# Lightning attention feeding a sine MLP: the start of the first chunk and the end of the second chunk's attention put in another order

## The chip, the cores and the metric

The kernel runs on one core of a Trainium2 chip. The time is what the device takes for one launch, in microseconds, as the median of several runs. Five engines work side by side, each through its own instructions in order: TensorE (PE, matmuls and transposes; PEld is its weight load), VectorE (DVE), ScalarE (ACT), GpSimd (POOL) and SyncE (SP). TensorE writes only to PSUM, eight banks of 2 KB per partition; DVE and ACT read results out of it. Transfers between memory and the on-chip buffers (SBUF) are issued from the queues of POOL and SP.

## What is computed

Block-wise linear attention over 4 batches x 8 heads x 768 positions x 64 values, with a decay per head, and then a two-layer MLP on the 3072 rows of 512 values that come out. Cut to what matters:

```python
for b in range(nb):                       # blocks of positions, state carried along
    intra = einsum('bhic,bhjc->bhij', qb, kb) * Dmask
    intra = einsum('bhij,bhjd->bhid', intra, vb)
    inter = einsum('bhid,bhde->bhie', qb * lam_pow, kv_state)
    out[:, :, sl] = intra + inter
    kv_state = lam_block * kv_state + einsum('bhsd,bhse->bhde', kb * rev_pow, vb)
x = out.transpose(0, 2, 1, 3).reshape(3072, 512)
h = x @ w_in                              # 512 -> 2048
g = h + sin(alpha * h)**2 / (alpha + 1e-09)
return g @ w_out                          # 2048 -> 512
```

## The kernel before

**Chunks and units.** The kernel takes 128 positions at a time: six chunks `t`, and four batches in each, so 24 units `u = 4*t + b`. Units 0 to 3 are the first chunk, 4 to 7 the second. The attention of chunk g+1 is worked in between the MLP of chunk g, so that both fill the engines.

**One unit's attention.** `transposes(u)` (L173) turns k and q with eight small matmuls, and ACT copies both out in one operation (`QKT`, L183). `scores(u)` (L196) makes k times q with eight matmuls into `F_ps` (two banks, tag `pf`), and DVE multiplies by the mask and writes `STm` (L209). `intra_mm(u)` (L244) multiplies `STm` with v into `O_ps`, `inter_mm(u)` (L254) adds the carried state, and `copy_x(u)` (L261, DVE) multiplies by the table `Etab` and writes the unit's columns of `xt`, the input of the MLP. `part_fo(uf, uo)` (L405) issues intra of `uo`, scores of `uf` and inter of `uo`, in this order. In the first chunk there is no carried state, and `first_out` (L345) stands in for intra, inter and copy.

**The MLP of one chunk** is cut into sixteen parts `f` of 128 columns. `hidden(g, f)` (L278) issues four matmuls of 512 columns into one bank, then ACT takes the sine (L286) and, for odd f and all f above 7 in chunk 0 and for every f later, the square (L289). `finish(g, f)` (L292) issues the DVE operation that makes `gall` (L296), which is also what frees the bank. `project(g, n)` (L305) is a quarter of an output tile, four matmuls of 512 columns: n runs over 16 pairs of (batch m, quarter), by `ORDER`. The first four of them come ahead of the next chunk's first `hidden`, the others between its parts. `hidden(1, 0)` reads `xt` of all four units 4 to 7.

**What sets the order.** The schedule is written by hand: each engine gets its instructions in the order in which the code issues them. `slots(0)` (L426) says after which `hidden(0, f)` which attention work of units 4 to 7 is issued, and the block under `if g == 0` (L503) issues what is left behind f = 15, with the first four `project` calls. `feed` (L452) does the same for POOL. PSUM banks go by tag: `pqk`, `po`, `ops`, `h0`, `h1`, `h2` of one bank each and `pf` of two; the next user of a tag waits for the reader of the one before. Chunk 0's hidden parts go through `FIRST` (`h0 h2 po h1 ops h0 h2 h1 ops` for f = 0 to 8) and then `h{f%3}`.

**The start.** k and q of unit 0 come through SP (`kraw`, `qraw`) and are cast by DVE (L334, L341). k, q and v of units 1 to 3 come through POOL's queue one by one (`load`, L85), then `w_in` in five pieces, then chunk 1 in halves (units 4 and 5, then 6 and 7). `spin(n)` (L356) issues n matmuls on a constant tile that nothing reads, into the bank of tag `h0`. `make_identity` (L110, L126) builds identity matrices with POOL; the small one, `idf`, serves the transpose of `alpha` (`a_ps`).

Of the kernel before, what the change touches and what calls it, by code (L numbers as in the profile page):

```python
# [15 lines left out]
def kernel(  # L16
# [15 lines left out]
    T = 128  # L32
# [90 lines left out]
            load(0, i, bi, bi + 1)  # L123
    load(0, 2, B - 1, B)
    idf = consts.tile([NFC, NFC], FP32, name="idf")
    make_identity(nc, idf[:])  # L126
    for i in range(4):
        load_w_in(i)
    new_chunk(1)
# [43 lines left out]
    def transposes(u, tag="pqk"):  # L173
        t, b = divmod(u, B)
        QK_ps = psA.tile([P, 2, HP, T], BF16, name="QK_ps", tag=tag)
        for hp in range(HP):
            nc.tensor.transpose(out=QK_ps[:, 1, hp, :],
                                in_=kn[t][:, b, 2 * hp:2 * hp + 2, :], identity=iden[:])
        for hp in range(HP):
            nc.tensor.transpose(out=QK_ps[:, 0, hp, :],  # L180
                                in_=qn[t][:, b, 2 * hp:2 * hp + 2, :], identity=iden[:])
        QKT = qkp.tile([P, 2, HP, T], BF16, name="QKT")
        nc.scalar.copy(out=QKT[:], in_=QK_ps[:])  # L183
        st[u]["QT"], st[u]["KT"] = QKT[:, 0, :, :], QKT[:, 1, :, :]
# [8 lines left out]
            for n in range(2):  # L193
                st[u + n][nm] = XT[:, n, :, :]

    def scores(u, halves=1):  # L196
        QT, KT = st[u]["QT"], st[u]["KT"]
        F_ps = psA.tile([P, 2, HP, T], FP32, name="F_ps", tag="pf")
        for hp in range(HP):
            for hd in range(2):  # L200
                nc.tensor.matmul(out=F_ps[:, hd, hp, :],  # L201
                                 lhsT=KT[hd * D:(hd + 1) * D, hp, :],
                                 rhs=QT[hd * D:(hd + 1) * D, hp, :],
                                 start=True, stop=True)
        STm = work.tile([P, 2, HP, T], BF16, name="STm")
        n = HP // halves
        for s in range(halves):
            w = slice(s * n, (s + 1) * n)
            nc.vector.tensor_tensor(out=STm[:, :, w, :], in0=F_ps[:, :, w, :], in1=Cmask[:, :, w, :],  # L209
                                    op=ALU.mult)  # L210
        st[u]["STm"] = STm

    def state_mm(us, tag="pqk"):
# [27 lines left out]
            nc.gpsimd.tensor_tensor(out=kvd[b][:], in0=kvs[u][:],  # L241
                                    in1=L128[:].unsqueeze(2).broadcast_to([P, HP, D]), op=ALU.mult)

    def intra_mm(u):  # L244
        t, b = divmod(u, B)
        O_ps = psA.tile([P, HP, T], FP32, name="O_ps", tag="po")
        for hp in range(HP):
            for hd in range(2):
                nc.tensor.matmul(out=O_ps[hd * D:(hd + 1) * D, hp, :],  # L249
                                 lhsT=vn[t][:, b, 2 * hp + hd, :], rhs=st[u]["STm"][:, hd, hp, :],  # L250
                                 start=(hp == 0), stop=False, skip_group_check=True)
        st[u]["O_ps"] = O_ps
# [8 lines left out]
    def copy_x(u):  # L261
        t, b = divmod(u, B)
        nc.vector.tensor_tensor(out=xt[t][:, :, b * T:(b + 1) * T], in0=st[u]["O_ps"][:], in1=Etab[:],  # L263
                                op=ALU.mult)
# [80 lines left out]
    def first_out(u, tag, hps_=range(4)):  # L345
        O_ps = psA.tile([P, HP, T], FP32, name="O_ps", tag=tag)
        for hp in hps_:
            for hd in range(2):
                nc.tensor.matmul(out=O_ps[hd * D:(hd + 1) * D, hp, :],
                                 lhsT=vn[0][:, u, 2 * hp + hd, :], rhs=st[u]["STm"][:, hd, hp, :],  # L350
                                 start=True, stop=True, skip_group_check=True)
        w = slice(hps_[0], hps_[-1] + 1)
        nc.vector.tensor_tensor(out=xt[0][:, w, u * T:(u + 1) * T], in0=O_ps[:, w, :],
                                in1=Etab[:, w, :], op=ALU.mult)

    def spin(n, cols=512):  # L356

        ps = psA.tile([P, GRP], FP32, name="hps", tag="h0")
        for _ in range(n):
            nc.tensor.matmul(out=ps[:, 0:cols], lhsT=fill[:, 0:P], rhs=fill[:, 0:cols], start=True, stop=True)  # L360

    spin(9)
    for nm, src, tag in (("KT", kn, "pqk"), ("QT", qn, "ops")):
        X_ps = psA.tile([P, HP, T], BF16, name="X_ps", tag=tag)
        for hp in range(HP):
            nc.tensor.transpose(out=X_ps[:, hp, :], in_=src[0][:, 0, 2 * hp:2 * hp + 2, :], identity=iden[:])
        XT = qkp.tile([P, HP, T], BF16, name=nm + "0")
        nc.scalar.copy(out=XT[:], in_=X_ps[:])
        st[0][nm] = XT[:]
        spin(3)  # L370
    scores(0)
    spin(1)
    transposes(1, "pqk")
    for hp in range(HP):
        nc.scalar.activation(out=Etab[:, hp, :], in_=pos_row[:], func=ACTF.Exp, scale=ln_hd[:, hp:hp + 1])
    spin(2)
    transposes(2, "ops")
    warm = consts.tile([P, 1], FP32, name="warm")
    nc.scalar.activation(out=warm[:], in_=lnlam[:, 0:1], func=ACTF.Sin)
    spin(1)  # L380
    scores(1)
    spin(1)
    first_out(0, "po")
    spin(1)
    scores(2)
    a_ps = psA.tile([P, NFC], FP32, name="a_ps", tag="h2")
    nc.tensor.transpose(out=a_ps[:], in_=alpha_fp[:], identity=idf[:])
    transposes(3, "pqk")
    spin(2)
    first_out(1, "h1")  # L390
    alpha_sb = consts.tile([P, NFC], FP32, name="alpha_sb")
    nc.vector.tensor_copy(out=alpha_sb[:], in_=a_ps[:])
    r_sb = consts.tile([P, NFC], FP32, name="r_sb")
    nc.vector.reciprocal(out=r_sb[:], in_=alpha_sb[:])
    spin(2)
    scores(3, 2)
    spin(1)
    first_out(2, "po")
    spin(2)
    first_out(3, "h1", range(0, 2))  # L400
    first_out(3, "ops", range(2, 4))
    spin(3)


    def part_fo(uf, uo, tag=None):  # L405

        if uo is not None:
            if tag:
                state_mm([uo], tag)
            intra_mm(uo)  # L410
        if uf is not None:
            scores(uf)
        if uo is not None:
            inter_mm(uo)
            if tag:
                state_put(uo)
                state_decay(uo)
# [8 lines left out]
    def slots(g):  # L426

        u = [B * (g + 1) + b for b in range(B)]
        T_, FO = transposes, part_fo
        if g == 0:  # L430
            return {3: [(part_k, (0, 1), "pf")], 6: [(part_k, (2, 3), "pf")],
                    7: [(T_, u[0])], 8: [(T_, u[1], "po")], 9: [(FO, u[0], None)],
                    11: [(FO, u[1], u[0]), (copy_x, u[0])], 12: [(T_, u[2])],
                    13: [(FO, None, u[1]), (T_, u[3], "ops"), (copy_x, u[1])], 14: [(FO, u[2], None)]}, {}
        if g == 1:
            return {4: [(part_k, (4, 5), h_tag(1, 5))], 6: [(part_k, (6, 7), h_tag(1, 7))],
                    8: [(FO, u[0], None)], 10: [(FO, u[1], u[0], h_tag(1, 11))],
                    12: [(FO, u[2], u[1], h_tag(1, 13))],
                    14: [(FO, u[3], u[2], h_tag(1, 15)), (copy_x, u[2])],
                    15: [(FO, None, u[3], h_tag(2, 0)), (copy_x, u[3])]}, {10: u[0], 12: u[1]}  # L440
        at = (3, 6, 9, 12, 14) if g == 2 else (1, 4, 7, 10, 13)
        tg = [h_tag(g, f + 1) if g < NT - 2 else None for f in at[1:]]
        return {at[0]: [(FO, u[0], None)], at[1]: [(FO, u[1], u[0], tg[0])], at[2]: [(FO, u[2], u[1], tg[1])],
                at[3]: [(FO, u[3], u[2], tg[2])], at[4]: [(FO, None, u[3], tg[3])]}, \
               {at[n + 1]: u[n] for n in range(4)}
# [30 lines left out]
    for g in range(NT + 1):  # L476
        if g < NT:
            gall[g] = gbp.tile([P, NFC, GRP], BF16, name="gall")
        at, xs = slots(g) if g + 1 < NT else ({}, {})
        fd = feed(g) if g + 1 < NT else {}  # L480
        if g + 1 < NT:
            new_xt(g + 1)
        for i in range(NFC):
            if g == NT and i >= NFC - 4 - LEAD:
                break
            for a in fd.get(i, []):
                if a is not None:
                    a[0](*a[1:])
            if g < NT:
                hidden(g, i)  # L490
            for a in at.get(i, []):
                a[0](*a[1:])
            if g > 0:
                n = i + LEAD
                if n < NFC:
                    project(g - 1, n)
                elif g < NT:
                    project(g, n - NFC)
            if g < NT:
                finish(g, i)  # L500
            if i in xs:
                copy_x(xs[i])
        if g == 0:  # L503

            project(0, 0)
            part_fo(7, 6)
            copy_x(6)
            project(0, 1)
            project(0, 2)
            part_fo(None, 7)  # L510
            copy_x(7)
            project(0, 3)
    project_halves(NT - 1, B - 1)

# [29 lines left out]
```

## Time and profile before

| what | us |
|---|---|
| median of 3 runs (lowest to highest) | 218.99 (218.78 to 219.08) |
| the profiled execution, its own time | 219.22 |
| its span on the core | 217.5 |
| PE busy | 208.3 (96%) |
| ACT busy | 147.2 (68%) |
| DVE busy | 126.6 (58%) |
| POOL busy | 94.3 (43%) |
| first matmul of hidden(0, 0) | at 18.48 |
| first matmul of hidden(1, 0) | at 46.26 |
| granted TensorE clock | 1.00 |

The times of the views count from the start of the span. A line of the timeline gives start, duration, engine, line of the kernel, operation, output and inputs with their shapes, how many were merged, and in brackets how long the engine stood idle before it and what ended that. A line of the chain gives start, duration and what it was; the chain is followed back from the last instruction, at each step to what released it. A line of the stretches gives the busy time of each engine with its number of instructions, the granted clock, and the transfers. A matmul's recorded duration holds its drain, so one following another starts before the first one's record ends.

### The profile page before, as it was taken

To read this page: it belongs to the slowest core of one execution; us is meant where nothing else is said; L and a number is where in the kernel's file an instruction comes from. 1 tells how busy PE (TensorE), PEld (TensorE's weight loads), DVE (VectorE), ACT (ScalarE), POOL (GpSimd) and SP (SyncE) were. 2 spreads that over 40 slices of the span, in tenths; PEclk is the share of its full clock that TensorE was granted. 3 is DMA by queue.
4 is the path that set the end of the run, shared out by engine and by line. 5 is a ranking of instruction groups with operands and counts; after the bars stand their busy time and mean duration, and the time that the engine had idled before them with its cause. 6 is when DMAs were issued, how large, how long until landed. Compare 5 with 4: busy or idle time off the path is not lost.

```text
span 217.5 us, 3864 instructions
## 1 busy us (share of the span) xinstructions
PE 208.3 (96%) x1504; PEld 99.6 (46%) x1504; DVE 126.6 (58%) x183; ACT 147.2 (68%) x234; POOL 94.3 (43%) x131
## 2 busy tenths in 40 slices
PE   7799986999999999999999999999999999999994
PEld 2354443544444544445454444444444444444453
DVE  4576977834656875567656777545767544444300
ACT  5573998728766648766667675777676779787521
POOL 7999999963899569052474611100000000000000
PEclk9999999999999999999999999999999999999999
DMA  5999999999999999929689990490110101111022
GB/s 102 150 158 198 176 167 184 208 175 154 197 176 136 177 148 139 189 46 135 143 101 124 166 119 29 116 128 21 75 50 3 48 0 48 51 50 48 0 101 96
DMA packets 99747, 24.65 MB, mean 113 GB/s; under 512 B 91904, under 2 KB 96784, under 8 KB 99728
## 3 DMA queue, kind: packets, MB, share of 16 engines
q0 software_dynamic: 76976, 13.37, 79.0%
q1 hardware_dynamic: 22752, 11.03, 23.6%
q8 instruction: 12, 0.20, 0.4%
q14 instruction: 7, 0.06, 0.1%
HBM read 27.28 MB, written 6.29 MB: 154 GB/s over the span
## 4 chain that ended last, share of the span: by engine, by line
PE 78%; POOL 10%; DMA 5%; ACT 2%; issue 2%; DVE 1%; POOLq 0%; ACTq 0%
PE ops L311 36%; PE hps L283 32%; DMA qn<-in_q_dram 5%; PE O_ps L257 3%; PE F_ps L201 2%; POOL vn L87 2%; PE O_ps L249 2%; POOL kdec L170 2%; POOL qn L87 2%; POOL w_in L93 2%; PE KVA_ps L220 2%; PE hps L325 2%; POOL kn L87 2%; ACT s_sb L286 1%; ACT s L289 1%
## 5 line engine op out<-in xcount | busy, mean ns | idle before, releaser
L296 DVE SCALAR_TENSOR_TENSOR gall<-s,r_sb,hps 128x512 bf16<-128x512 bf16 x96 | 71.2, 745 | 67.0 <-ACT s L289 66.7
L286 ACT ACTIVATE s_sb<-hps,alpha_sb 128x512 bf16<-128x512 f32 x96 | 65.8, 687 | 49.7 <-PE hps L283 49.7
L283 PE MATMUL hps<-xt,w_in 128*128 128x512 bf16 x384 | 97.6, 379 | 0.1
L311 PE MATMUL ops<-w_out,gall 128*128 128x512 bf16 x368 | 93.0, 379 | 0.0
L289 ACT ACTIVATE s<-s_sb 128x512 bf16<-128x512 bf16 x92 | 58.0, 630 | 3.0
L283 PEld LDWEIGHTS <-w_in 128*128 128x128 bf16 x384 | 36.9, 98 | 44.3 <-DVE kvs L229 0.9
L311 PEld LDWEIGHTS <-gall 128*128 128x128 bf16 x368 | 34.8, 98 | 38.3
L235 POOL CAST kv<-kvs 64x256 bf16<-64x256 f32 x40 | 16.0, 401 | 41.8 <-PE O_ps L257 36.8
L209 DVE TENSOR_TENSOR STm<-F_ps,Cmask 128x1024 bf16<-128x1024 f32 (+1 forms) x25 | 29.4, 1178 | 3.8 <-PE F_ps L201 3.1
L170 POOL TENSOR_TENSOR kdec<-kn,Rtok 128x512 bf16<-128x512 bf16 x20 | 20.9, 1065 | 2.8 <-DMA kn<-in_k_dram 2.5
L316 ACT COPY o_sb<-ops 128x512 f32<-128x512 f32 x23 | 13.2, 572 | 6.4 <-PE ops L311 6.4
L263 DVE TENSOR_TENSOR xt<-O_ps,Etab 128x512 bf16<-128x512 f32 x20 | 13.7, 684 | 1.7 <-PE O_ps L257 1.6
L87 POOL DMA_DIRECT2D vn<-in_v_dram x12 | 14.2, 1195 | 0.0
L87 POOL DMA_DIRECT2D kn<-in_k_dram x11 | 13.5, 1227 | 0.3 <-issue 0.3
L87 POOL DMA_DIRECT2D qn<-in_q_dram x11 | 13.3, 1206 | 0.0
L360 PE MATMUL hps<-fill 128*128 128x512 bf16 x31 | 10.8, 455 | 1.5 <-DVE fill L112 1.5
L241 POOL TENSOR_TENSOR kvd<-kvs,L 128x256 f32<-128x256 f32 x16 | 9.8, 615 | 1.0
L249 PE MATMUL O_ps<-STm,vn 128*64 128x128 bf16 x160 | 8.0, 222 | 1.1 <-DVE STm L209 0.6
L183 ACT COPY QKT<-QK_ps 128x1024 bf16<-128x1024 bf16 x7 | 7.0, 1002 | 2.0 <-PE QK_ps L180 1.9
L249 PEld LDWEIGHTS <-vn 128*64 128x64 bf16 x160 | 5.3, 110 | 4.5 <-issue 3.5
L220 PEld LDWEIGHTS <-kdec 128*64 128x64 bf16 x160 | 3.8, 111 | 6.8 <-issue 6.4
L201 PE MATMUL F_ps<-QT,KT 64*128 64x128 bf16 x136 | 6.8, 219 | 0.0
(61 smaller groups left out, 84.5 us busy)
## 6 DMA issues: line engine op xcount, KB each, us to landing
out_dram<-o_sb SPq DMA_DIRECT2D x23, 256.0 KB, 2.7
w_out<-in_moe_w_out_dram POOLq DMA_DIRECT2D x4, 512.0 KB, 14.0
w_in<-in_moe_w_in_dram POOLq DMA_DIRECT2D x3, 512.0 KB, 9.5
kn<-in_k_dram POOLq DMA_DIRECT2D x6, 256.0 KB, 10.9
qn<-in_q_dram POOLq DMA_DIRECT2D x6, 256.0 KB, 11.3
vn<-in_v_dram POOLq DMA_DIRECT2D x6, 256.0 KB, 11.3
kn<-in_k_dram POOLq DMA_DIRECT2D x2, 512.0 KB, 7.5
qn<-in_q_dram POOLq DMA_DIRECT2D x2, 512.0 KB, 8.5
```

What stands on the lines that cost most here:

```text
L87: nc.gpsimd.dma_start(out=dst[t][:, b0:b1, :, :].rearrange("p b h e -> p (b h) e"), in_=src[b0:b1, :, t * T:(t + 1) * T, :].rearrange("b h ...
L170: nc.gpsimd.tensor_tensor(out=kdec[:], in0=kn[t][:, b, :, :], in1=head_bc(Rtok), op=ALU.mult)
L209: nc.vector.tensor_tensor(out=STm[:, :, w, :], in0=F_ps[:, :, w, :], in1=Cmask[:, :, w, :], op=ALU.mult)
L235: nc.gpsimd.tensor_copy(out=kv[b][s, :, hd, :], in_=kvs[u][s, :, :])
L249: nc.tensor.matmul(out=O_ps[hd * D:(hd + 1) * D, hp, :], lhsT=vn[t][:, b, 2 * hp + hd, :], rhs=st[u]["STm"][:, hd, hp, :], start=(hp == 0) ...
L263: nc.vector.tensor_tensor(out=xt[t][:, :, b * T:(b + 1) * T], in0=st[u]["O_ps"][:], in1=Etab[:], op=ALU.mult)
L283: nc.tensor.matmul(out=hps[:], lhsT=w_in_of[f][:, c, :], rhs=xt[g][:, c, :], start=(c == 0), stop=(c == NDC - 1))
L286: nc.scalar.activation(out=s_sb[:], in_=hps[:], func=ACTF.Sin, scale=alpha_sb[:, f:f + 1])
L289: nc.scalar.activation(out=s2[:], in_=s_sb[:], func=ACTF.Square)
L296: nc.vector.scalar_tensor_tensor(out=gall[g][:, f, :], in0=s2[:], scalar=r_sb[:, f:f + 1], in1=hps[:], op0=ALU.mult, op1=ALU.add)
L311: nc.tensor.matmul(out=ops[:], lhsT=gall[g][:, f, m * P:(m + 1) * P], rhs=w_out_sb[part][:, f % 4, :], start=(f == 0), stop=(f == NFC - 1))
L316: nc.scalar.copy(out=o_sb[:], in_=ops[:])
```

## The change

There are four edits.

1. The small identity `idf` is no longer built by POOL (two instructions, behind the loads of chunk 0 and ahead of the `w_in` loads) but copied by DVE out of the large one, behind `tri`'s memset and ahead of the four memsets of `kv`.
2. In the first chunk, units 1 and 3 turn k and q apart (`half_T`: four transposes into one bank, one ACT copy of 512 columns, for each), as unit 0 did already; unit 2 stays with `transposes`. Unit 1's scores are issued ahead of unit 2's transposes; `alpha`'s transpose, its copy and the reciprocal move ahead of `scores(1)`; the load of the sine's table moves behind the copies of unit 3; and `first_out(2)` goes ahead of `scores(3)`, so that on DVE the third x is written ahead of unit 3's masked scores. 28 fill matmuls stand where 31 did.
3. In `slots(0)` the attention of units 4 to 7 moves to later slots. The transposes of units 6 and 7 both come behind `hidden(0, 14)`, with the intra and inter of unit 5, whose O goes to the bank `ops`.
4. Behind `hidden(0, 15)` and its `finish`: scores of 6 and of 7 first (7's in the banks `h1` and `h2`, masked by two DVE operations of 512 columns), then intra, inter and copy of 6, two `project` calls, intra (in bank `h0`), inter and copy of 7, two `project` calls.

```diff
     idf = consts.tile([NFC, NFC], FP32, name="idf")
-    make_identity(nc, idf[:])
+    nc.vector.tensor_copy(out=idf[:], in_=iden[0:NFC, 0:NFC])
...
-    def scores(u, halves=1):
+    def scores(u, halves=1, tags=None):
         QT, KT = st[u]["QT"], st[u]["KT"]
-        F_ps = psA.tile([P, 2, HP, T], FP32, name="F_ps", tag="pf")
+        if tags:
+
+            F = [psA.tile([P, 1, HP, T], FP32, name="F_ps", tag=tag) for tag in tags]
+            parts = [(F[hd][:], (slice(hd, hd + 1), slice(0, HP))) for hd in range(2)]
+            F_of = [F[hd][:, 0] for hd in range(2)]
...
+        for src, (x, w) in parts:
+            nc.vector.tensor_tensor(out=STm[:, x, w, :], in0=src, in1=Cmask[:, x, w, :], op=ALU.mult)
...
-    def intra_mm(u):
+    def intra_mm(u, bank="po"):
...
+    def half_T(u, nm, tag):
+
+        src = {"KT": kn, "QT": qn}[nm]
         X_ps = psA.tile([P, HP, T], BF16, name="X_ps", tag=tag)
         for hp in range(HP):
-            nc.tensor.transpose(out=X_ps[:, hp, :], in_=src[0][:, 0, 2 * hp:2 * hp + 2, :], identity=iden[:])
+            nc.tensor.transpose(out=X_ps[:, hp, :], in_=src[0][:, u, 2 * hp:2 * hp + 2, :], identity=iden[:])
         XT = qkp.tile([P, HP, T], BF16, name=nm + "0")
         nc.scalar.copy(out=XT[:], in_=X_ps[:])
-        st[0][nm] = XT[:]
-        spin(3)
+        st[u][nm] = XT[:]
+
+    spin(9)
+    half_T(0, "KT", "pqk")
+    spin(3)
+    half_T(0, "QT", "ops")
+    spin(1)
+    half_T(1, "KT", "pqk")
+    spin(1)
     scores(0)
-    spin(1)
-    transposes(1, "pqk")
+    half_T(1, "QT", "ops")
...
+    spin(2)
+    scores(1)
+    spin(1)
+    transposes(2, "pqk")
+    spin(1)
+    first_out(0, "po")
+    spin(1)
+    scores(2)
+    spin(2)
+    half_T(3, "KT", "ops")
+    spin(1)
+    first_out(1, "h1")
+    half_T(3, "QT", "h2")
...
+    spin(1)
+    first_out(2, "po")
     scores(3, 2)
-    spin(1)
-    first_out(2, "po")
-    spin(2)
+    spin(3)
     first_out(3, "h1", range(0, 2))
     first_out(3, "ops", range(2, 4))
-    spin(3)
+    spin(2)
...
-                    7: [(T_, u[0])], 8: [(T_, u[1], "po")], 9: [(FO, u[0], None)],
-                    11: [(FO, u[1], u[0]), (copy_x, u[0])], 12: [(T_, u[2])],
-                    13: [(FO, None, u[1]), (T_, u[3], "ops"), (copy_x, u[1])], 14: [(FO, u[2], None)]}, {}
+                    8: [(T_, u[0])], 9: [(T_, u[1], "po")], 10: [(FO, u[0], None)],
+                    12: [(FO, u[1], u[0]), (copy_x, u[0])],
+                    14: [(FO, None, u[1], None, "ops"), (copy_x, u[1]), (T_, u[2]), (T_, u[3], "po")]}, {}
...
         if g == 0:
 
+            scores(6)
+            scores(7, 1, ("h1", "h2"))
+            part_fo(None, 6)
+            copy_x(6)
             project(0, 0)
-            part_fo(7, 6)
-            copy_x(6)
             project(0, 1)
+            part_fo(None, 7, None, "h0")
+            copy_x(7)
             project(0, 2)
-            part_fo(None, 7)
-            copy_x(7)
             project(0, 3)
```

More of the change, by code (lines that the diff above doesn't have):

```diff
@@ L194, in dma_transposes @@
                 st[u + n][nm] = XT[:, n, :, :]
-    def scores(u, halves=1):
+    def scores(u, halves=1, tags=None):
         QT, KT = st[u]["QT"], st[u]["KT"]
-        F_ps = psA.tile([P, 2, HP, T], FP32, name="F_ps", tag="pf")
+        if tags:
+            F = [psA.tile([P, 1, HP, T], FP32, name="F_ps", tag=tag) for tag in tags]
+            parts = [(F[hd][:], (slice(hd, hd + 1), slice(0, HP))) for hd in range(2)]
+            F_of = [F[hd][:, 0] for hd in range(2)]
+        else:
+            F_ps = psA.tile([P, 2, HP, T], FP32, name="F_ps", tag="pf")
+            n = HP // halves
+            ws = [slice(s * n, (s + 1) * n) for s in range(halves)]
+            parts = [(F_ps[:, :, w, :], (slice(0, 2), w)) for w in ws]
+            F_of = [F_ps[:, hd] for hd in range(2)]
         for hp in range(HP):
             for hd in range(2):
-                nc.tensor.matmul(out=F_ps[:, hd, hp, :],
+                nc.tensor.matmul(out=F_of[hd][:, hp, :],
                                  lhsT=KT[hd * D:(hd + 1) * D, hp, :],
@@ L205, in scores @@
         STm = work.tile([P, 2, HP, T], BF16, name="STm")
[L206 to L210, printed above, removed]
+        for src, (x, w) in parts:
+            nc.vector.tensor_tensor(out=STm[:, x, w, :], in0=src, in1=Cmask[:, x, w, :], op=ALU.mult)
         st[u]["STm"] = STm
@@ L242, in state_decay @@
                                     in1=L128[:].unsqueeze(2).broadcast_to([P, HP, D]), op=ALU.mult)
-    def intra_mm(u):
+    def intra_mm(u, bank="po"):
         t, b = divmod(u, B)
-        O_ps = psA.tile([P, HP, T], FP32, name="O_ps", tag="po")
+        O_ps = psA.tile([P, HP, T], FP32, name="O_ps", tag=bank)
         for hp in range(HP):
@@ L360, in spin @@
             nc.tensor.matmul(out=ps[:, 0:cols], lhsT=fill[:, 0:P], rhs=fill[:, 0:cols], start=True, stop=True)
-    spin(9)
-    for nm, src, tag in (("KT", kn, "pqk"), ("QT", qn, "ops")):
+    def half_T(u, nm, tag):
+        src = {"KT": kn, "QT": qn}[nm]
         X_ps = psA.tile([P, HP, T], BF16, name="X_ps", tag=tag)
         for hp in range(HP):
-            nc.tensor.transpose(out=X_ps[:, hp, :], in_=src[0][:, 0, 2 * hp:2 * hp + 2, :], identity=iden[:])
+            nc.tensor.transpose(out=X_ps[:, hp, :], in_=src[0][:, u, 2 * hp:2 * hp + 2, :], identity=iden[:])
         XT = qkp.tile([P, HP, T], BF16, name=nm + "0")
         nc.scalar.copy(out=XT[:], in_=X_ps[:])
-        st[0][nm] = XT[:]
-        spin(3)
+        st[u][nm] = XT[:]
[6 more added lines that the diff above has]
+    spin(1)
     scores(0)
-    spin(1)
-    transposes(1, "pqk")
+    half_T(1, "QT", "ops")
     for hp in range(HP):
         nc.scalar.activation(out=Etab[:, hp, :], in_=pos_row[:], func=ACTF.Exp, scale=ln_hd[:, hp:hp + 1])
-    spin(2)
-    transposes(2, "ops")
-    warm = consts.tile([P, 1], FP32, name="warm")
-    nc.scalar.activation(out=warm[:], in_=lnlam[:, 0:1], func=ACTF.Sin)
-    spin(1)
[L381 to L385, printed above, removed]
     a_ps = psA.tile([P, NFC], FP32, name="a_ps", tag="h2")
     nc.tensor.transpose(out=a_ps[:], in_=alpha_fp[:], identity=idf[:])
-    transposes(3, "pqk")
-    spin(2)
-    first_out(1, "h1")
     alpha_sb = consts.tile([P, NFC], FP32, name="alpha_sb")
@@ L395, with part_fo @@
     spin(2)
-    scores(3, 2)
+    scores(1)
[10 more added lines that the diff above has]
+    half_T(3, "QT", "h2")
+    warm = consts.tile([P, 1], FP32, name="warm")
+    nc.scalar.activation(out=warm[:], in_=lnlam[:, 0:1], func=ACTF.Sin)
     spin(1)
     first_out(2, "po")
-    spin(2)
+    scores(3, 2)
+    spin(3)
     first_out(3, "h1", range(0, 2))
     first_out(3, "ops", range(2, 4))
-    spin(3)
-    def part_fo(uf, uo, tag=None):
+    spin(2)
+    def part_fo(uf, uo, tag=None, bank="po"):
         if uo is not None:
@@ L409, in part_fo @@
                 state_mm([uo], tag)
-            intra_mm(uo)
+            intra_mm(uo, bank)
         if uf is not None:
```

## The prediction, as it was written before the changed kernel ran

> **What bounds the kernel now.** First I asked from when on PE is full, by the busy time of two stretches (from, to, length, then PE, PEld, DVE, ACT, POOL):
>
> ```profile
> 36.10:46.26 10.16, 9.64 (x92) 5.06 (x93) 7.74 (x10) 5.56 (x8) 10.07 (x12) 1.00 1.36 202
> 46.26:214.20 167.94, 167.94 (x1153) 80.22 (x1151) 92.80 (x128) 115.68 (x184) 49.75 (x69) 1.00 0.87 99
> ```
>
> From 46.26, the start of hidden(1, 0), PE is busy 167.94 of 167.94 us, and the same work lies behind that point in both kernels. So **the change is worth exactly the shift of hidden(1, 0)**. What sets it is read from the chain of waits up to there:
>
> ```profile
> 24.34 11.70 DMA qn<-in_q_dram
> ...
> 36.51 0.89 ACT QKT L183
> ...
> 41.54 0.64 ACT s L289
> ...
> 42.87 1.22 DVE STm L209
> 44.09 0.61 DVE xt L263
> ...
> 44.74 0.41 PE O_ps L249 x8
> 45.15 0.33 PE O_ps L257 x4
> ```
>
> q of units 6 and 7 lands at 36.03; then ACT's copies, sines and squares to 42.17; then DVE. The timeline shows which of these engines was really full:
>
> ```profile
> 26.54 0.69 ACT L286 ACTIVATE s_sb<-hps,alpha_sb 128x512 bf16<-128x512 f32 x1 [0.28 <-PE hps L283]
> ...
> 36.08 0.40 PE L180 MATMUL QK_ps<-iden,qn 128*128 128x128 bf16 x4 [1.17 <-DMA qn<-in_q_dram]
> ...
> 36.51 1.01 ACT L183 COPY QKT<-QK_ps 128x1024 bf16<-128x1024 bf16 x1 [0.61 <-PE QK_ps L180]
> ...
> 42.21 0.75 DVE L296 SCALAR_TENSOR_TENSOR gall<-s,r_sb,hps 128x512 bf16<-128x512 bf16 x1 [0.49 <-ACT s L289]
> 42.87 1.22 DVE L209 TENSOR_TENSOR STm<-F_ps,Cmask 128x1024 bf16<-128x1024 f32 x1
> 44.01 0.68 DVE L263 TENSOR_TENSOR xt<-O_ps,Etab 128x512 bf16<-128x512 f32 x1
> ...
> 45.52 0.69 DVE L263 TENSOR_TENSOR xt<-O_ps,Etab 128x512 bf16<-128x512 f32 x1 [0.83 <-PE O_ps L257]
> ```
>
> PE waits 1.17 for q, ACT only 0.61: between 26.54 and 42.17 ACT is idle for nothing else. **ACT bounds this stage, and behind its last square DVE does.** Behind 42.17 come gall 15 (to 42.87), the masked scores of 7 (to 44.01), copy 6 (to 44.70), PE's intra and inter of 7 (to 45.5), copy 7 (to 46.21): 4.09 from the end of the square to hidden(1, 0).
>
> **The change part by part.**
>
> *Start.* What ends last before hidden(0, 0) is DVE:
>
> ```profile
> 16.09 1.22 DVE L209 TENSOR_TENSOR STm<-F_ps,Cmask 128x512 bf16<-128x512 f32 x2
> 17.23 1.34 DVE L353 TENSOR_TENSOR xt<-O_ps,Etab 128x512 bf16<-128x512 f32 x3
> ```
>
> The last x ends at 18.57. After: q of unit 2 still lands at 10.92 (issued 6.12, 4.8 to landing), turned by 11.31 (0.40), copied by ACT to 12.35 (1.0), scores to 12.82 (0.42), masked on DVE to 14.07 (1.22), x of 1 to 14.75 (0.68). v of unit 2 lands at about 14.7 (issued 9.59, 5.1), so first_out(2) ends at 15.15 and x of 2 runs 15.20 to 15.87. Then unit 3's masked scores to 17.09, PE's second half to 17.5, the last half x to 17.92: **0.65 earlier**. From below 0.2, by which unit 3's mask alone starts sooner (16.09 to 15.87), from above 1.7, as w_in's first piece lands at 16.8 (issued 11.72, 5.1) and bars anything sooner.
>
> Costs around it: the DVE copy of idf waits for POOL's identity (3.95) and holds the four kv memsets (1.09) and ln_hd (0.34) behind it; the copy itself costs at most the 0.17 of alpha's, eight times as large, so the cast of unit 0's k ends at about 6.0 instead of 5.58. The cover is qraw, landing at 6.5: the transposes of q start at 7.32 either way. Without it the 0.4 would count in full. POOL loses two instructions (0.37 from 11.32) and issues w_in 0.37 sooner; the transfers are back to back (busy 9 tenths in every slice), so landings move by 0 to 0.37, and none of them is what is waited for: nothing. Halved copies cost ACT 0.59 twice against 1.0, in idle time; alpha's copy and reciprocal (0.17 + 0.25) fit between unit 0's mask (to 10.05) and the scores of 1 (10.5); the sine's table (1.28) loads from 15.0 and is there long before the first sine at 18.9; three fill matmuls fewer, nothing.
>
> *Slots.* With units 6 and 7 turned behind hidden(0, 14), PE reaches them at 36.4: q is there, and the 1.17 and 0.46 (for k) of PE's waiting go. ACT gains only its 0.61. From hidden 7 on, ACT's work is the same number of sines, squares and copies, in another order, so its last square ends at 42.17 - 0.65 - 0.61 = **40.91**. Cover for the moved work: DVE now does the mask of 4 behind gall 9 and ahead of gall 10, so gall 10 ends near 33.5 and hidden 13, which takes its bank, is ready at 34.6, while ACT asks for it at 35.2. Below 0.6 lost there nothing shows; above it each us counts.
>
> *Tail.* The finish of 15 is issued ahead of scores(6), and DVE works in order, so **the masked scores of 6, before done at 40.93, now stand behind gall 15**, and PE's intra of 6 behind them, with all four project calls behind that. After 40.91: gall 15 0.04 + 0.66; masked scores 1.22, to 42.83; 0.05; intra and inter of 6 0.34 + 0.24 (as at 41.42 and 42.09); two projects 1.73 (42.33 to 44.06); intra and inter of 7 0.55; two projects 1.73. Sum 6.56, so hidden(1, 0) starts at 47.47. Copy 7 ends by 46.6 beside the last projects, and 7's mask in two halves (1.22 for two in the row above) ends by 44.0: both covered. Before, a project was done ahead of intra 6 and two more during DVE's work; now PE has nothing from about 39.8 to 42.85. The tail costs 6.56 - 4.09 = 2.47 more, and the gains are 1.26.
>
> **Sum: 47.47 - 46.26 = +1.2 us**: 219.22 + 1.2 = 220.4 for the profiled execution, which stands 0.23 above the median; 220.2 for the median.
>
> *The PE clock.* The nine first matmuls show what a cold array costs:
>
> ```profile
> 1.52 4.02 PE L360 MATMUL hps<-fill 128*128 128x512 bf16 x9 [1.52 <-DVE fill L112]
> ```
>
> They start 0.43 apart (4.02 less one drain), the fills at 17.60 0.21 (three in 0.82, of which the drain is some 0.4): 9 x 0.21 = 1.9 us lost. The new gap of 3.0 us is longer than any here (1.17 left the matmuls at full rate). So from both sides: nothing, by the gap of 1.17, or 1.9, by this row. I take nothing: 0.66 us of score matmuls lie just ahead of the gap.
>
> The Trainium skill (TensorE: Matmul & The Clock Gate, "HAM oscillation — how this bites in real kernels") speaks against the change: no idle gaps of PE above some 3.4 us, or the array falls to half rate. The 3.0 is short of it; were the rule's edge crossed, its window at half rate would cost 1.7, and the sum would be +2.9. No row before shows it.
>
> **The rivals.**
>
> *Faster: PE's waits are the price.* If PE bounded this stage, the waits would come back whole: 0.65 + 1.17 + 0.46 = 2.3, time 216.7. For it: PE is 96% busy, and the chain goes through q's landing. Against: ACT's queue. It decides if the last square ends by 40.91 - 1.21 = 39.7; then hidden(1, 0) is no later than before. Only a start 1.2 sooner than I have it gives that.
>
> *No change.* The start moves by the most that w_in allows, 1.7: the square ends at 39.9, the sum is +0.2, time 219.2. Against it: x of 2 now waits for v.
>
> *Slower, by more: the start brings nothing.* v of 2 lands 0.65 later or the kv memsets reach past qraw; then hidden(1, 0) is at 48.1, and the time 220.85.
>
> *Clock.* +1.2 + 1.9: 222.1.
>
> **How the numbers follow.** Forecast (+0.7 to +1.65, the start at its lower bound: 219.7 to 220.65) 0.62; faster 0.09; no change 0.07; slower by more 0.13; clock 0.09. Predicted 220.2. The range leaves out the faster case and the far end of the clock, 219.3 to 221.3. A difference under 0.2% (0.44 us) can't be told from none in this kernel; by the cases faster 0.09, same 0.07, slower 0.84.
>
> **What would show it.** Right: hidden(0, 0) near 17.85; no wait for q at units 6 and 7; ACT without a gap from hidden 7 to its last square, near 40.9; then gall 15 and masked scores of 6 on DVE back to back; PE idle about 3 us before intra 6, released by DVE; hidden(1, 0) near 47.5 with PE full after it. Wrong: masked scores of 6 ahead of gall 15; the square done by 39.7; PE gaps behind hidden(1, 0); fills or projects 0.43 apart after the gap.

## The result, and the profile after

The changed kernel takes 223.95 us (223.87 to 223.98, 4 runs) against 218.88 of the kernel before in the same session: ratio 1.0231, 95% interval 1.0214 to 1.0249. It is slower, as forecast, but by 5.1 us where 1.2 was predicted, and outside the range. The profiled execution has a span of 222.2, 4.7 longer than before.

The stretches show where it lies. The columns are from:to, length, busy time of PE, PEld, DVE, ACT and POOL with their instructions, the granted clock, and the transfers.

```profile
41.84:44.65 2.81, 0.05 (x2) 0.08 (x1) 1.93 (x3) 0.81 (x2) 2.79 (x4) 1.00 1.24 208
44.65:48.65 4.00, 3.78 (x20) 1.81 (x21) 1.83 (x3) 0.00 (x0) 1.73 (x3) 0.58 2.17 168
48.65:50.95 2.30, 2.30 (x21) 1.27 (x21) 0.69 (x1) 0.00 (x0) 1.20 (x2) 1.00 2.58 163
50.95:218.90 167.95, 166.74 (x1132) 80.21 (x1151) 92.85 (x128) 115.59 (x184) 47.80 (x67) 1.00 0.80 95
```

PE has nothing for 2.8 us, then runs 4.00 us at a granted clock of 0.58, and is full from 50.95, the start of hidden(1, 0). That point stood at 46.26, so the shift is 4.69; what follows takes 171.25 to the end of the span, and took 171.24 before.

The timeline gives the steps between (start, duration, engine, line, operation, tiles, count, and what ended the idle time before):

```profile
37.88 0.41 PE L256 MATMUL O_ps<-STm,vn 128*64 128x128 bf16 x8
...
41.49 0.40 PE L211 MATMUL F_ps<-QKT 64*128 64x128 bf16 x8 [0.52 <-ACT QKT L183]
44.65 0.64 PE L256 MATMUL O_ps<-STm,vn 128*64 128x128 bf16 x8 [2.77 <-DVE STm L217]
...
48.65 0.41 PE L256 MATMUL O_ps<-STm,vn 128*64 128x128 bf16 x8
```

Intra 6 (the third of these) is recorded with 0.64 for its eight matmuls, intra 5 and intra 7 with 0.41: the array is at half rate behind the gap and back at full rate 4 us later. What intra 6 waited for is on DVE and ACT:

```profile
42.05 0.63 ACT L296 ACTIVATE s<-s_sb 128x512 bf16<-128x512 bf16 x1
...
42.72 0.75 DVE L303 SCALAR_TENSOR_TENSOR gall<-s,r_sb,hps 128x512 bf16<-128x512 bf16 x1 [1.73 <-ACT s L296]
43.38 2.41 DVE L217 TENSOR_TENSOR STm<-F_ps,Cmask 128x1024 bf16<-128x1024 f32 x3
```

ACT's last square ends at 42.68, gall 15 follows, and the masked scores of 6 stand behind it, as the prediction had it. That square is not 1.26 earlier than before, though, but 0.51 later, because the stage began late. The timeline of the start, of the changed kernel:

```profile
1.52 4.02 PE L367 MATMUL hps<-fill 128*128 128x512 bf16 x9 [1.52 <-DVE fill L112]
6.41 0.61 PE L374 MATMUL X_ps<-iden,kn 128*128 128x128 bf16 x4 [0.88 <-DVE kn L341]
6.81 1.49 PE L367 MATMUL hps<-fill 128*128 128x512 bf16 x3
8.09 0.63 PE L374 MATMUL X_ps<-iden,qn 128*128 128x128 bf16 x4
...
10.48 0.40 PE L374 MATMUL X_ps<-iden,qn 128*128 128x128 bf16 x4
```

Before, the transposes of unit 0's k started at 5.63 and were at full rate (0.40 for four). Here they come at 6.41, and groups of four take 0.6, three fills 1.49 (0.81 before), until past 9.9. hidden(0, 0) starts at 19.72 instead of 18.48.

| step | predicted | measured |
|---|---|---|
| start of hidden(0, 0) | -0.65 | +1.24 |
| from there to the last square | -0.61 | -0.73 |
| from the square to hidden(1, 0), order of the work | +2.47 | +2.48 |
| the same, matmuls at half rate (4.00 for intra 6 to the second project, 2.31 by the prediction's sum) | 0 | +1.70 |
| sum | +1.2 | +4.69 |

The table holds for the profiled run, whose mean granted clock was 0.992. The other three runs of the changed kernel took the same time at 0.985. In tail_only and idf_late, below, a run at 0.985 was some 1.0 us longer than one at 0.992. So in these three the half rate behind the gap probably lasted longer and the array was probably warm early at the start; there is no trace of them, and how their 5 us divide is not shown.

### The profile page after: what moved, and what is told of

Read it like the earlier page. It is cut to its first block, busy times and chain, and to the rows that moved or that the text cites. A ratio compares the mean times of both kernels' runs of the same rounds, so it can differ in the third digit from the quotient of the medians.

```text
span 222.2 us, 3832 instructions
## 1 busy us (share of the span) xinstructions
PE 209.1 (94%) x1475; PEld 101.3 (46%) x1501; DVE 126.9 (57%) x185; ACT 147.4 (66%) x236; POOL 93.7 (42%) x129
## 4 chain that ended last, share of the span: by engine, by line
PE 85%; ACT 5%; issue 4%; DVE 3%; POOL 1%; ACTq 0%; POOLq 0%
PE ops L318 36%; PE hps L290 34%; PE F_ps L211 3%; PE O_ps L264 3%; ACT s_sb L293 3%; PE O_ps L256 2%; PE KVA_ps L227 2%; ACT QKT L183 2%; PE hps L367 2%; DVE STm L217 2%; PE hps L332 2%; PE X_ps L374 1%; ACT s L296 1%; DVE kv L136 0%; PE O_ps L356 0%
## 5 line engine op out<-in xcount | busy, mean ns | idle before, releaser
L318 PE MATMUL ops<-w_out,gall 128*128 128x512 bf16 x352 | 91.3, 382 | 1.0 <-issue 0.4
L242 POOL CAST kv<-kvs 64x256 bf16<-64x256 f32 x40 | 16.0, 400 | 46.3 <-PE O_ps L264 36.9
L211 PE MATMUL F_ps<-QT,KT 64*128 64x128 bf16 x152 | 7.8, 223 | 0.5 <-DVE alpha_sb L393 0.4
L236 DVE TENSOR_TENSOR kvs<-KVA_ps,kvd 128x256 f32<-128x256 f32 x16 | 6.6, 422 | 0.1
```

The costliest lines, as they stand in the source:

```text
L211: nc.tensor.matmul(out=F_of[hd][:, hp, :], lhsT=KT[hd * D:(hd + 1) * D, hp, :], rhs=QT[hd * D:(hd + 1) * D, hp, :], start=True, stop=True)
L242: nc.gpsimd.tensor_copy(out=kv[b][s, :, hd, :], in_=kvs[u][s, :, :])
L318: nc.tensor.matmul(out=ops[:], lhsT=gall[g][:, f, m * P:(m + 1) * P], rhs=w_out_sb[part][:, f % 4, :], start=(f == 0), stop=(f == NFC - 1))
```

## The experiments

All stand on the changed kernel unless said otherwise. Ratios are to the kernel before, run in the same session.

| run | median us | ratio (95% interval) |
|---|---|---|
| undo_idf | 225.58 | 1.0283 (1.0253 to 1.0314) |
| idf_late | 223.54 | 1.0190 (1.0151 to 1.0230) |
| fill_gap | 221.40 | 1.0092 (1.0055 to 1.0128) |
| proj_gap | 219.33 | 1.0014 (0.9995 to 1.0034) |
| start_only | 219.70 | 1.0038 (1.0025 to 1.0052) |
| tail_only | 222.68 | 1.0183 (1.0160 to 1.0206) |
| gap_half | 221.33 | 1.0124 (1.0103 to 1.0146) |
| late_proj | 219.24 | 1.0012 (0.9999 to 1.0024) |
| stm6_first | 219.07 | 1.0005 (0.9988 to 1.0022) |
| act0_proj | 218.72 | 0.9987 (0.9972 to 1.0002) |
| best | 218.13 | 0.9958 (0.9945 to 0.9971) |
| best_act0 | 217.87 | 0.9943 (0.9927 to 0.9958) |

**Which half of the change carries it: start_only and tail_only.** start_only is the kernel before with edits 1 and 2, tail_only with edits 3 and 4.

> The kernel before with edits 1 and 2 alone (the new start), slots and tail as before. Theory: the new start is worth nothing by itself here, as the transposes of unit 6 wait for q at 36.03 anyway: with full rate from about 6.4 hidden(0, 0) starts near 17.9 and hidden(1, 0) stays near 46.3, time near 218.9; with half rate until about 10 hidden(0, 0) starts near 19.7 and 0.6 of the 1.24 is left behind the wait, time near 219.6. Rival (the start carries most of the 5 us): above 222.

> The kernel before with edits 3 and 4 alone (slots and tail), start as before. Theory (the tail carries it): ACT's last square ends near 41.6 (no wait for q), then the same 8.3 us to hidden(1, 0) as in the changed kernel with its idle gap and half rate, 49.8, time near 222.6, more if the half rate lasts longer. Rival (the start carries it): within 1.3 of before, 220.2.

tail_only took 222.68, with hidden(1, 0) at 49.60 and a granted clock of 0.992 over the span, as its theory said: **the tail carries most of the loss**. start_only took 219.70. Its profiled run was at full rate early and started hidden(0, 0) at 17.93, and yet hidden(1, 0) came at 46.83, 0.57 later than before. The expectation had 46.3 for this case, so something takes the earlier start back and more. In its trace PE waits 0.69 for `w_in` at 20.50 and 1.26 for q of unit 4 at 28.63; behind the second ACT has its longest wait of the stage, 0.86. So here it is the transfers.

**The gap and the clock: fill_gap, gap_half, proj_gap.** Fill matmuls ahead of intra 6, 12 or 6 of them (`spin` takes a tag for it), or the first three project calls:

```diff
             scores(7, 1, ("h1", "h2"))
+            spin(12, 512, "pqk")      # fill_gap; gap_half: spin(6, 512, "pqk")
             part_fo(None, 6)
```

```diff
+            project(0, 0)
+            project(0, 1)
+            project(0, 2)
             part_fo(None, 6)
             copy_x(6)
-            project(0, 0)
-            project(0, 1)
             part_fo(None, 7, None, "h0")
             copy_x(7)
-            project(0, 2)
             project(0, 3)
```

> The changed kernel with 12 fill matmuls (2.6 us at full rate) issued ahead of intra 6, where TensorE stood idle 2.77 us; nothing reads them. Theory (the gap cools the array): the granted clock stays at 1.00, intra 6 to the second project take 2.3 us instead of 4.0, and the time falls by 1.7 to 222.3. Rival (the matmuls behind the gap are slow through contention with DVE or the transfers): they stay 0.43 apart and the time stays at 223.9.

> The changed kernel with 6 fill matmuls behind the scores of 7 instead of 12, so that some 1.5 us of the idle gap are left. Theory (an idle stretch as long as 2.8 us cools the array, one of 1.5 does not, as the kernel before keeps its rate through 1.17): granted clock 1.00, time as with 12 fills, 221.4. Rival (any gap of this order does it by the chance of the window): half rate in some or all runs, 222.5 to 224.

> The changed kernel with the first three project calls issued ahead of intra 6, so that the gap holds real work. Theory (gap and clock): w_out is there (landed by 42.3 before), intra 6 still starts near 44.65 at full rate, copy 7 ends near 47.3, hidden(1, 0) starts near 47.3 instead of 50.95, time near 220.3. Rival (clock lost for another reason): half rate behind 44.65, hidden(1, 0) near 49, time near 222. Rival (DVE's tail is not what holds): hidden(1, 0) before 46.5, time below 219.5.

With matmuls that nothing reads, the kernel is 2.5 us faster. The timeline of fill_gap:

```profile
40.97 2.76 PE L367 MATMUL hps<-fill 128*128 128x512 bf16 x12
43.81 0.41 PE L256 MATMUL O_ps<-STm,vn 128*64 128x128 bf16 x8
44.15 0.40 PE L264 MATMUL O_ps<-QKT,kv 128*128 128x128 bf16 x4
44.39 1.89 PE L318 MATMUL ops<-w_out,gall 128*128 128x512 bf16 x8
46.21 0.41 PE L256 MATMUL O_ps<-STm,vn 128*64 128x128 bf16 x8
```

Intra 6 to intra 7 takes 2.40 instead of 4.00, beside the same work on DVE and no less transfer (195 GB/s against 168), so contention is out. Measured in this way the half rate cost 1.6. (Between the two profiled runs the other 0.8 comes from the start: in fill_gap's the array was at full rate from 6.4.) Six fills do as well: in gap_half's profile 1.37 us of the gap are left and the clock stays at 1.00. One of its four runs took 222.34, 1.0 more than the others, at a mean clock of 1.00 as well. The gap there is shorter, but dense matmuls also lie just ahead of it; the two are not told apart.

proj_gap puts real work there. In its profiled run (220.21) hidden(1, 0) starts at 47.25 (47.3 expected); the median, 219.33, is lower than the 220.3 expected, and the time is that of the kernel before within its interval. From the last square to hidden(1, 0) 4.65 us pass, 8.27 in the changed kernel and 4.09 in the kernel before: **idle PE and half rate together made up 3.6 of the 4.2 us that the tail lost.**

**What makes the gap: stm6_first.** Only gall 15 is issued later:

```diff
-            if g < NT:
+            if g < NT and (g, i) != (0, 15):
                 finish(g, i)
...
             scores(6)
+            finish(0, 15)
             scores(7, 1, ("h1", "h2"))
```

> The changed kernel with only one DVE operation moved: the finish of part 15 (gall 15) is issued behind the scores of 6 instead of ahead of them. Theory (DVE's order makes the gap): the masked scores of 6 run at about 40.2 to 41.2, before gall 15; intra 6 starts within a us of the scores of 7, TensorE has no idle stretch over 1.2 us there, the granted clock stays 1.00, hidden(1, 0) starts near 46.2 (47.0 where the start is at half rate), time 219.2 to 220. Rival (TensorE waits for something else there): the gap and the half rate stay, 223 and more.

The timeline of stm6_first, DVE and PE:

```profile
39.94 1.23 DVE L217 TENSOR_TENSOR STm<-F_ps,Cmask 128x1024 bf16<-128x1024 f32 x1
41.65 0.75 DVE L303 SCALAR_TENSOR_TENSOR gall<-s,r_sb,hps 128x512 bf16<-128x512 bf16 x1 [0.48 <-ACT s L296]
```

```profile
40.42 0.40 PE L211 MATMUL F_ps<-QKT 64*128 64x128 bf16 x8 [0.52 <-ACT QKT L183]
41.22 0.41 PE L256 MATMUL O_ps<-STm,vn 128*64 128x128 bf16 x8 [0.41 <-DVE STm L217]
```

The mask of 6 now runs while ACT is still on part 15, the gap of 2.77 is one of 0.41, the clock is 1.00, and hidden(1, 0) starts at 45.93. One instruction moved on DVE takes the median from 223.95 to 219.07. Up to 0.9 of that is a start at full rate in most of its runs (hidden(0, 0) at 17.93 in the profile); its three slowest runs of ten lie at 219.74 to 220.10, still 3.9 below. That DVE's order made the gap is shown.

**The start: undo_idf, idf_late, late_proj.**

```diff
-    nc.vector.tensor_copy(out=idf[:], in_=iden[0:NFC, 0:NFC])
+    make_identity(nc, idf[:])          # undo_idf
```

In idf_late and late_proj the same DVE copy is issued behind the mask table `Cmask` instead, ahead of the first masked scores; late_proj also has proj_gap's order of the tail.

> The changed kernel with only edit 1 undone: the small identity is built by POOL again. Theory (the start): the DVE copy of it held the kv memsets and so the cast of unit 0's k; TensorE then stood idle 0.88 us behind its first nine matmuls (0.1 before), stayed at half rate until 10.4 instead of 5.6, and that made hidden(0, 0) 1.24 later. So here the matmuls are at full rate from about 5.6, hidden(0, 0) starts near 17.9 (19.72 in the changed kernel), everything to the last square moves by some 1.8, the gap ahead of intra 6 and the half rate behind it stay, and the time is near 222.1. Rival (chance of the window, or the new order of the start costs it): half rate until about 10 again, hidden(0, 0) near 19.7, time near 223.9.

> The changed kernel with the DVE copy of the small identity kept, but issued behind the mask table instead of ahead of the kv memsets. Theory: it is the place on DVE and not the engine that costs; full rate from about 5.6, hidden(0, 0) near 17.9 to 18.1, time near 222.1, as with edit 1 undone. Rival (POOL's two instructions less, and so earlier loads, are what disturbs the start): as the changed kernel, 223.9.

> Three projects in the gap, and the small identity copied by DVE behind the mask table. The three projects alone gave times near 219.27 in most runs and near 220.3 in some, and the profile of a run with 220.2 showed half rate until 10.2. Theory (the idle 0.88 us behind the first nine matmuls leaves it to chance whether the array warms at 5.5 or near 10): here the cast comes in time, every run is at full rate from 5.6, all times lie near 219.2 and none near 220.3. Rival (chance of the window alone, gap or not): the same two groups of times.

undo_idf failed for a reason that I had overlooked: edit 2 moves alpha's transpose up in PE's queue, and POOL builds the identity only behind the loads of chunk 0. The timeline of undo_idf:

```profile
8.70 0.40 PE L374 MATMUL X_ps<-iden,qn 128*128 128x128 bf16 x4
11.72 0.23 PE L391 MATMUL a_ps<-idf,alpha_fp 16*128 16x16 f32 x1 [2.62 <-POOL idf masks.py:199]
11.89 1.03 PE L367 MATMUL hps<-fill 128*128 128x512 bf16 x2
12.85 0.61 PE L211 MATMUL F_ps<-QT,KT 64*128 64x128 bf16 x8
```

Edits 1 and 2 belong together. As a side effect this shows the gap and the clock a second time: 2.62 us idle, and half rate behind it until about 15.

idf_late had hidden(0, 0) at 18.00, where 17.9 to 18.1 was expected, but its time was 223.54, not 222.1: hidden(1, 0) came at 49.95. Only 1.0 of the 1.72 us won at the start arrived there: at 26.93 ACT waits 1.15 for a matmul, where the changed kernel has 0.28 (more below). Its four runs lie at 222.92 and 223.08 with a mean clock of 0.992, and at 224.00 and 224.08 with 0.985, so the half rate behind the gap probably also lasts longer in some runs than in others. Three of tail_only's lie at 222.41 to 222.79 with 0.991 and 0.992, the fourth at 223.65 with 0.985.

Whether the array is warm after the first nine fills is not fixed by the 0.88 us of idle time alone: fill_gap has the same start and was at full rate from 6.43 in its profile, the changed kernel and proj_gap only from about 10.4. proj_gap's ten times are seven from 219.26 to 219.49 and three from 220.21 to 220.32; the profiled one, with the late start, is among the latter. late_proj, where the cast comes in time, has all eleven between 219.22 and 219.46, as expected. It is not proof: of the thirty runs of act0_proj, best and best_act0, which have the same start, two (219.97 and 219.38) stand some 1.2 above their medians, and no trace says why.

**Where the earlier start goes: act0_proj.** late_proj with part 0's square on ACT instead of DVE:

```diff
     def on_act(g, f):
-        return f % 2 == 1 or f > 7 if g == 0 else True
+        return f % 2 == 1 or f > 7 or f == 0 if g == 0 else True
```

> late_proj with the square of part 0 given to ACT. There this square took DVE 2.01 us (0.42 for the same operation later) beside POOL's decay of k, and the chain of gall and banks behind it made ACT wait 0.57 and 0.34 for matmuls. Theory (that collision is what eats the earlier start): both waits fall under 0.2, ACT's last square ends near 41.2 instead of 41.6 although ACT has one square (0.54) more, time near 218.9. Rival (the collision costs nothing on the path): ACT's chain is longer by the square, time near 219.8.

The reason for it was this pair in late_proj's timeline, POOL and DVE:

```profile
17.25 4.16 POOL L169 TENSOR_TENSOR kdec<-kn,Rtok 128x512 bf16<-128x512 bf16 x4
```

```profile
19.69 2.01 DVE L301 TENSOR_TENSOR s<-s_sb 128x512 bf16<-128x512 bf16 x1 [1.91 <-ACT s_sb L292]
21.74 1.41 DVE L302 SCALAR_TENSOR_TENSOR gall<-s,r_sb,hps 128x512 bf16<-128x512 bf16 x2
```

The square, 0.42 where it has DVE to itself, ends 0.3 behind POOL's last decay of k. In the kernel before it started 0.57 later and took 0.87, and ended 0.9 ahead of POOL's last decay, so it does not always wait for that one; in the changed kernel's profile it started at 21.50, when POOL was almost through, and took 0.43. With the square on ACT, ACT's waits of over 0.2 for matmuls in this stage shrink from 0.57 and 0.34 to one of 0.28, its last square ends at 41.20 instead of 41.61, and the time falls from 219.24 to 218.72. The medians agree with the theory (218.9) and not with the rival (219.8), but the intervals of the two runs (0.9972 to 1.0002 and 0.9999 to 1.0024) just touch.

The expectation read the 0.57 wrongly, though. late_proj's PE shows what that matmul had waited for:

```profile
22.50 2.76 PE L289 MATMUL hps<-xt,w_in 128*128 128x512 bf16 x12 [0.60 <-DMA w_in<-in_moe_w_in_dram]
```

It was a transfer, which in act0_proj's trace was there in time. So the two traces differ in two things, and the pair does not give the price of the square. The pair of the next section, best and best_act0, does: the start of both is late_proj's, and in neither trace is PE seen to wait for `w_in` there.

**A version that beats both: best and best_act0.** The copy of the identity behind `Cmask`, and this tail (the loop leaves out the finish of part 15, as in stm6_first):

```diff
             scores(6)
+            project(0, 0)
             scores(7, 1, ("h1", "h2"))
+            project(0, 1)
             part_fo(None, 6)
             copy_x(6)
-            project(0, 0)
-            project(0, 1)
-            part_fo(None, 7, None, "h0")
+            part_fo(None, 7, None, "pf")
             copy_x(7)
+            finish(0, 15)
             project(0, 2)
             project(0, 3)
```

> The changed kernel with all that the runs so far point to: the identity copied behind the mask table; behind part 15 the masked scores of 6 and 7 and the copies of x ahead of gall 15 on DVE; two projects among the scores and two behind intra and inter of 7 (whose O goes to the freed pair of banks). Theory: TensorE is full from the scores of 6 on and hidden(1, 0) starts near 45.0 to 45.3, time near 218.0, faster than both. Rival (ACT or w_out holds it): hidden(1, 0) near 46.2 again, 219.2.

> The same with the square of part 0 on ACT. If the collision of DVE and POOL costs on the path, 217.6; if not, 218.5.

The timeline of best:

```profile
39.95 2.58 DVE L216 TENSOR_TENSOR STm<-F_ps,Cmask 128x1024 bf16<-128x1024 f32 x3
42.88 1.37 DVE L269 TENSOR_TENSOR xt<-O_ps,Etab 128x512 bf16<-128x512 f32 x2 [0.36 <-PE O_ps L263]
44.16 0.74 DVE L302 SCALAR_TENSOR_TENSOR gall<-s,r_sb,hps 128x512 bf16<-128x512 bf16 x1
```

Both masks and both copies of x are done before gall 15, hidden(1, 0) starts at 45.08 (45.0 to 45.3 expected), and the ratio is 0.9958 (0.9945 to 0.9971; one of its twelve runs, at 219.38, is not explained).

The same trace has the price of the square, on PE and on ACT:

```profile
25.09 0.44 PE L226 MATMUL KVA_ps<-vn,kdec 128*64 128x64 bf16 x16 [0.48 <-DVE kvs L233]
```

```profile
26.71 0.69 ACT L292 ACTIVATE s_sb<-hps,alpha_sb 128x512 bf16<-128x512 f32 x1 [1.01 <-PE hps L289]
```

The late square makes DVE's copies of the state (`kvs`) late, PE waits 0.48 for them, and ACT 1.01 for the hidden part behind. In best_act0 PE's wait is gone, ACT's is 0.28, as in the kernel before, and ACT's last square ends at 41.06 instead of 41.61. But hidden(1, 0) comes at 45.01, only 0.07 sooner: there PE waits 0.41 for w_out ahead of the first project, so the transfers are the next thing in the way. The ratio is 0.9943 (0.9927 to 0.9958); the median, 217.87, lies nearer to the theory's 217.6 than to 218.5, but the two intervals overlap, so that the square costs ACT time is shown, and that it costs time of the kernel is not.

## Why the prediction was wrong, point by point

- **Everything hangs on hidden(1, 0): right.** 171.25 us lie behind it after, 171.24 before.
- **Slots, 0.61 won on ACT: right.** 0.73 measured, and 0.70 in tail_only, which has the old start; no wait for q is left at units 6 and 7.
- **Tail, 6.56 from the last square: right in its order.** gall 15, mask of 6, intra 6 at 1.97 behind the square (1.97 by the sum), and in fill_gap, at full rate, 6.67 from the square to hidden(1, 0). stm6_first shows the cause.
- **The PE clock, "I take nothing": this step failed, for 1.6 to 1.7 us in the profiled run.** (1.6 by fill_gap, 1.7 by the sum.) The cost from the first nine fills was sized well for that run (1.9 as the upper bound), but the choice between the bounds was wrong: the 0.66 us of score matmuls ahead of the gap did not keep the array warm. A gap of 2.8 us did cool it in the profile; one of 1.4, with dense fills ahead of it, did not. The nearest row (1.17) was less than half as long, and taking its value went beyond what it could say. fill_gap shows it. The page of the Trainium skill that was weighed there (TensorE: Matmul & The Clock Gate, "HAM oscillation — how this bites in real kernels") puts the edge at about 3.4 us of idle time; the gaps of 2.62 and 2.77 read above were shorter and cost the rate all the same, so the measurement decides.
- **The start, "0.65 earlier": this step failed in the profiled run, for 1.9 us.** The cover that was named, qraw at 6.5, covers the data but not the array. The cast of unit 0's k took 0.82 (0.43 before) and ended at 6.35, where about 6.0 was reckoned; PE stood idle 0.88 behind its fills and, in this run, stayed at half rate until 10.4. In fill_gap, with the same idle 0.88 but full rate from 6.43, the transposes of q start at 7.31, as reckoned (7.32), and hidden(0, 0) at 17.94. So the rate made the delay, and the late cast alone did not. The fills are there to warm the array, and I had counted them as work with no effect. What decides between the two rates is open.
- **That an earlier start reaches ACT whole: failed too.** With the array warm, hidden(0, 0) starts at 17.9 as worked out (17.93 in start_only, 17.94 in fill_gap, 18.00 in idf_late), but ACT's last square in fill_gap and idf_late ends at 41.84, not at 40.91. The square of part 0 on DVE meets POOL's decay of k, and ACT's wait at 26.9 is 1.15 in idf_late and 0.73 in fill_gap instead of 0.28; best_act0 shows it go with the square. In idf_late this is nearly all: from hidden(0, 0) to the last square it takes 0.88 more than the changed kernel. In fill_gap, with 0.94 more, it is half; a wait of 0.30 for w_in is in its trace too, and the rest is not settled.
- **The rivals.** Clock (222.1, chance 0.09) and a start that brings nothing (220.85, chance 0.13) came together, which the list of single cases did not allow for; their sum is +1.2 + 0.65 + 1.9 and more.

## What to carry to other kernels

An instruction put ahead of another on an in-order engine is a wait for all that stand behind it: before work is moved, list what the other engine has in its queue at that point (here one finish ahead of one mask made some 4 us). A gap that opens on PE costs its own length and, where it was as long as 2.6 us here, the rate of the matmuls behind it, so fill it with work that is ready. Keeping the warm-up matmuls running up to the first real ones is a precaution: with 0.88 us between them the rate came out both ways. An earlier start is won only if the engines that run beside it at the new time are not in its way.

## What the runs showed of the hardware

- 2.62 and 2.77 us without matmuls halved the rate behind them, for some 3.5 to 4 us in the profiles; 1.17 us and, with six fills just ahead, 1.37 us did not. Between them no run measured. The rate need not fall at the end of the gap: in tail_only intra 6, behind 2.77 us, is still recorded with 0.41, and the matmuls slow down some 0.4 us later.
- The half rate of the very first matmuls (0.43 apart) is not in the granted clock, which reads 1.00 there; the half rate behind a gap is (0.58 in the changed kernel).
- Whether nine fills were enough to warm the array after an idle 0.88 us differed between runs of the same start: full rate at 6.4 or only at about 10.4.
- A bf16 square of 128x512 took DVE 2.01 us beside POOL's bf16 products in late_proj and best, and 0.42 to 0.43 alone. That one held the other up is argued from their times; no run measured the pair by itself.
